# Seven products for both projections of the last two token tiles of a bilinear FFN

## The chip, the cores and the metric

One core of a Trainium2 chip runs the whole program. The metric is the device time of one execution in microseconds. Of the kernel before there are three timed runs: 325.77, 326.64 and 326.76 us, median 326.64. One further execution was taken by the profiler.

The core has a matrix engine (TensorE, PE in the profile), a vector engine (VectorE, DVE), a scalar engine (ScalarE, ACT), a general engine (GpSimd, POOL) and a queue engine (SyncE, SP) that issues transfers. Matmuls write to PSUM, eight banks of 128 partitions by 2 KB. VectorE and ScalarE read PSUM; in this kernel GpSimd works on SBUF only.

## The reference

Two stages, of which only the second is touched. The first is attention over 8 batches, 8 heads, 576 positions and head size 64, with a local mask for four heads and a strided mask for the other four. Its output, as a matrix x of 4608 tokens by 512, goes through a bilinear feed-forward layer:

```
a = x @ w_a          # 4608 x 512 times 512 x 1536
b = x @ w_b          # the same shape
out = (a * b) @ w_out   # 4608 x 1536 times 1536 x 512, float32
```

## The kernel before, in words

**Tiles and slots.** The tokens are cut into nine tiles of 512 (t = 0 to 8). A tile has sixteen slots: twelve for the blocks f = 0 to 11 of 128 features (`ffn_ab`), in which a and b of a block are made and multiplied into `pf[:, f]`, and four for the output product with w_out (`ffn_y` in tiles 0 and 1, `ffn_ys` in tiles 2 to 8). The attention of batch b + 1 is woven into the slots of the feed-forward tiles, and ends in the output slots of tile 6. Tiles 7 and 8 are feed-forward alone.

**Order.** The order of the work on each engine is the order in which the program is written out; nothing reorders it. A loop over the slots calls the slot's function, then what is due at that slot: entries put down with `do(slot, function, ...)`. Where a slot has such entries, a one-element copy on GpSimd (`pace`, line 1054) reads the slot's result, which holds GpSimd's queue back to about that slot.

**A plain block.** `ab_mm` (line 623) makes a and b in two PSUM banks by 4 matmuls of 512 columns each; ScalarE copies a to SBUF (line 644), and VectorE multiplies the copy with b out of PSUM into `pf` (line 647). The banks come from `mm_bank`: three banks with the tag mm and one with the tag tp, every fourth request going to tp. A bank of a tag is handed on in the order in which the banks of that tag came free. Four further banks serve the attention (`o` and `st`, two banks each).

**Seven products in place of eight.** The output product has been made this way since earlier versions: a 2 x 2 block matrix product with seven block products and some sums of blocks (Winograd's form of Strassen's scheme). `fast_w` makes the sums of w_out, `fast_s` (line 755) the sums of `pf` in `ps`, and `y_plan` (line 809) or, in the last tile, `y_tail` (line 838) makes the products 1 to 7 in three PSUM places X, Y, Z: 1, 6, 5 and 3 add up in X, 7 and 4 in Z, 2 stands in Y. ScalarE copies what stands there after 1, 7, 6, 5 and 3, VectorE adds after 4 and 2.

**The first projection in seven products.** Tiles 7 and 8 use the scheme for a alone as well, in four pairs of blocks each (`FAST_A`, `a_pair`, lines 700 to 735): a pair of blocks (2 x 128 features) by two halves of the tile (2 x 256 tokens) by two halves of the contraction. A product is then two matmuls of 256 columns (line 700). The b of the pair is made plainly (line 707), and VectorE multiplies both blocks at the end of the pair (line 712). The sums of w_a come from `wsum_make` (line 664; eight VectorE instructions of 768 elements, in tile 6's slots 2, 4, 6 and 8), the sums of x from `xsum_make` (line 674; one ahead of tile 7, three in its first slot, four in its output slots for tile 8). They stand in buffers that the attention has finished with. X of a pair is in the `st` or `o` banks.

**Columns of pf.** In tiles 2 to 8 the product is written into `pf` with its columns permuted, so that the two halves of the output scheme are blocks of sixteen tokens; the store puts the rows back in place.

Of the kernel before, what the change touches and what calls it, by code (L numbers as in the profile page):

```python
# [16 lines left out]
RS = 8  # L17
# [10 lines left out]
FAST_A = {7: (1, 2, 3, 4), 8: (0, 1, 2, 3)}  # L28
# [3 lines left out]
def kernel(  # L32
# [29 lines left out]
    pst = ctx.enter_context(tc.tile_pool(name="pst", bufs=1, space=bass.MemoryType.PSUM))  # L62
# [23 lines left out]
    vs_buf = [const.tile([NP, HL, RS, VW], BF16, name=f"vs{i}") for i in range(2)]  # L86
# [291 lines left out]
    def S_p(b, u):  # L378
# [3 lines left out]
        st = pst.tile([128, 2, 512], F32, tag="st", name="st")  # L382
# [243 lines left out]
    def ffn_ab(t, f, mid, ab=None):  # L626
        if f == 0:
            pfs[t] = fsb.tile([128, FD, TTOK], BF16, tag="pf", name="pf", bufs=1)
        pf = pfs[t]
        if f // 2 in FAST_A.get(t, ()):  # L630
            if f % 2 == 0:
                pairs[t, f // 2] = a_pair(t, f // 2)
            return next(pairs[t, f // 2])
        if ab is None:
            ab = [mm_bank([128, TTOK]) for _ in range(2)]
            if f == 0:

                late = 1 if t == 1 else 3
                ab_mm(t, f, ab, [kk for kk in range(KD) if kk != late], last=-1)
                ab_mm(t, f, ab, [late], first=-1, last=late)  # L640
            else:
                ab_mm(t, f, ab, range(KD), mid)
        a_sb = fsb.tile([128, TTOK], F32, tag="a_sb", name="a_sb")
        nc.scalar.copy(a_sb, ab[0])  # L644
        if t in FAST_Y:
            halves = lambda x: x.rearrange("p (a i s) -> p a i s", i=2, s=16)
            nc.vector.tensor_mul(pf[:, f, :].rearrange("p (i a s) -> p a i s", i=2, s=16), halves(a_sb), halves(ab[1]))  # L647
        else:
            nc.vector.tensor_mul(pf[:, f, :], a_sb, ab[1])  # L649
        return pf[:1, f, :1]  # L650

    wav = wa_sb.rearrange("p (j c) (g e m) -> p j c g e m", c=2, e=2, m=128)
    wsum_a = [flat.rearrange("p (c g m) -> p c g m", c=2, g=FG)
              for flat in [vl_buf[0].rearrange("p a b -> p (a b)")[:, 12 * 128 * z:12 * 128 * (z + 1)] for z in range(2)]
              + [t.rearrange("p a b c -> p (a b c)")[:, :12 * 128] for t in qz_pair[0]]]
    xsum = {t: qz_pair[1][t - 7].rearrange("p a b c -> p (a b c)")[:, :8 * HT].rearrange("p (n c m) -> p n c m", n=4, c=2)
            for t in FAST_A}

    def wsum_make(n):
        w, s_ = (lambda e, j: wav[:, j, :, :, e]), wsum_a  # L660
        a, b, op = ((w(1, 0), w(1, 1), ALU.add), (s_[0], w(0, 0), ALU.subtract), (w(0, 0), w(1, 0), ALU.subtract),
                    (w(0, 1), s_[1], ALU.subtract))[n]
        for c in range(2):
            nc.vector.tensor_tensor(s_[n][:, c], a[:, c], b[:, c], op=op)
# [11 lines left out]
    pairs = {}  # L676

    def a_pair(t, g):

        pf = pfs[t]  # L680
        pool, nm = ((pst, "st"), (psum4["o"], "o"))[g % 2]
        X = pool.tile([128, 2, 512], F32, tag=nm, name="ax")[:, 0, :HT]
        a = ([fsb.tile([128, TTOK], F32, tag="a_sb", name="a_sb") for _ in range(2)] if g % 2 == 0 else
             [t.rearrange("p h n -> p (h n)")[:, :2 * TTOK].bitcast(F32) for t in kT_buf[0]])
        got = {k: psum4[nm].tile([128, TTOK], F32, tag=nm, name="mm")
               for k, nm in zip((1, "Z", "Y", 0), (("mm", "mm", "tp", "mm"), ("tp", "mm", "mm", "mm"))[g % 2])}
        Z, Y = got["Z"][:, :HT], got["Y"][:, :HT]
        p7 = fsb.tile([128, HT], F32, tag="p7", name="p7")
        quarter = lambda e, k: a[e][:, HT * k:HT * (k + 1)]
        w = lambda e, j: (lambda c: wav[:, j, c, g, e])  # L690
        ws = lambda n: (lambda c: wsum_a[n][:, c, g])
        x = lambda j, k: (lambda c: x_part(t, j, k)[:, c])
        xs = lambda n: (lambda c: xsum[t][:, n, c])
        plan = {"1": (X, w(0, 0), x(0, 0)), "2": (Y, w(0, 1), x(1, 0)), "3": (X, ws(3), x(1, 1)), "4": (Z, w(1, 1), xs(3)),
                "5": (X, ws(0), xs(0)), "6": (X, ws(1), xs(1)), "7": (Z, ws(2), xs(2))}

        def P(k):
            bank, lhs, rhs = plan[k]
            for c in range(2):
                nc.tensor.matmul(bank, lhsT=lhs(c), rhs=rhs(c), start=k in "172" and c == 0, stop=c == 1, skip_group_check=True)  # L700

        x0 = TTOK * t % (XR * S)

        def b_mm(e, kks):
            f = 2 * g + e
            for kk in kks:
                nc.tensor.matmul(got[e], lhsT=wb_sb[:, kk, 128 * f:128 * (f + 1)], rhs=xT[:, kk, x0:x0 + TTOK],  # L707
                                 start=kk == 0, stop=kk == KD - 1)

        def mult(e):  # L710
            halves = lambda v_: v_.rearrange("p (a i s) -> p a i s", i=2, s=16)
            nc.vector.tensor_mul(pf[:, 2 * g + e, :].rearrange("p (i a s) -> p a i s", i=2, s=16),
                                 halves(a[e]), halves(got[e]))

        P("1")
        nc.scalar.copy(quarter(0, 0), X)
        b_mm(1, (0, 1, 2))
        P("6")
        nc.scalar.copy(quarter(1, 0), X)
        b_mm(1, (3,))  # L720
        P("7")
        nc.scalar.copy(p7, Z)
        P("2")
        nc.vector.tensor_tensor(quarter(0, 0), Y, quarter(0, 0), op=ALU.add)
        yield None
        P("5")
        nc.scalar.copy(quarter(1, 1), X)
        nc.gpsimd.tensor_tensor(quarter(1, 1), quarter(1, 1), p7, op=ALU.add)
        if (t, g - 1) in later:
            later.pop((t, g - 1))()  # L730
        b_mm(0, (0, 1))
        P("4")
        nc.vector.tensor_tensor(quarter(1, 0), Z, quarter(1, 0), op=ALU.add)
        P("3")
        nc.scalar.copy(quarter(0, 1), X)
        b_mm(0, (2, 3))
        mult(1)
        mult(0)
        yield pf[:1, 2 * g + 1, :1]

    later = {}
# [3 lines left out]
    def fast_s(t, n, gs):  # L745
# [6 lines left out]
        if (t, n) == (NT - 1, 2) and {gs.start, gs.start + 1} <= set(FAST_A[t]):  # L752
            later[t, gs.start] = lambda: nc.gpsimd.tensor_tensor(s[:, n], a, b, op=op)
            return
# [18 lines left out]
    def y_store(eng, t, y, i, q, n=slice(0, d_model)):  # L773
        rows = out[TTOK * t:TTOK * (t + 1), n].rearrange("(a i s q) c -> a s i q c", i=2, s=8, q=2)
        eng.dma_start(out=rows[:, :, i, q], in_=y[i][:, q, n])
# [18 lines left out]
    Y_ORDER = [(x[0], int(x[1])) for x in "10 11 70 71 60 61 40 41 50 51 20 21 30 31".split()]  # L794
    TAIL_ORDER = [(x[0], int(x[1])) for x in "10 70 60 11 40 50 71 30 61 20 51 41 31 21".split()]

    def y_plan(t):

        plan, y = products(t), y_bufs()
        bank = {x: mm_bank([128, 2, HN]) for x in "ZXY"}  # L800

        def store_half(i):
            rows = out[TTOK * t:TTOK * (t + 1)].rearrange("(a i s q) c -> a s i (q c)", i=2, s=8, q=2)
            nc.sync.dma_start(out=rows[:, :, i], in_=y[i].rearrange("p q c -> p (q c)"))

        for n, (k, q) in enumerate(Y_ORDER):
# [14 lines left out]
    def y_tail(t):  # L821

        plan, y = products(t), y_bufs()
        banks = [{x: mm_bank([128, HN]) for x in "ZXY"},
                 {"X": psum4["o"].tile([128, 2, 512], F32, tag="o", name="end")[:, 0, :HN],
                  "Z": pst.tile([128, 2, 512], F32, tag="st", name="end")[:, 0, :HN]}]
        for k, q in TAIL_ORDER:
# [4 lines left out]
            for n in cuts:  # L832
                if (q, k) == (1, "2"):
                    bank = mm_bank([128, 128])
# [10 lines left out]
                if k == "54"[q]:  # L845
                    y_store(nc.sync, t, y, 1, q)
                elif (q, k) == (0, "2"):
# [7 lines left out]
    def ffn_ys(t, j, mid):  # L855
# [9 lines left out]
        return (y[0][:1, 0, :1], None, y[1][:1, 0, HN:HN + 1], y[1][:1, 0, :1])[j]  # L865
# [36 lines left out]
    with tc.manual_schedule(engines={ENG.PE, ENG.SP, ENG.Pool, ENG.DVE, ENG.Activation}):  # L902
        early = ExitStack()
        open_psum(early, tp=2, sum=1, misc=1, o=2)
# [28 lines left out]
        for nm in ORDER:  # L933
# [26 lines left out]
            elif nm[0] == "F":  # L960
                f = int(nm[1])
                if nm[2] == "A":
                    if f == 1:
                        ab = pst.tile([128, 2, 512], F32, tag="st", name="ab")
# [10 lines left out]
        open_psum(ctx, mm=3, tp=1, o=1)  # L975
# [17 lines left out]
        for t in FAST_Y[:-1]:  # L993
# [7 lines left out]
        for b in range(FIRST_D, B):  # L1001
# [15 lines left out]
            for (z, nm, part), g in zip(((0, "k", 0), (0, "k", 1), (0, "q", 0), (0, "q", 1), (1, "k", 0), (1, "k", 1),  # L1017
                                         (1, "k", 2), (1, "q", 0), (1, "q", 1), (1, "q", 2)), gs):
                if (b, z, nm, part) != (FIRST_D, 0, "k", 1):
                    do(g0 + g, step_D, b, z, nm, part)  # L1020
        for n in range(4):
            do(16 * (NT - 3) + 2 * n + 2, wsum_make, n)
        do(16 * (NT - 2) - 1, xsum_make, NT - 2, 0)
        for n in (2, 1, 3):
            do(16 * (NT - 2), xsum_make, NT - 2, n)
        for n in range(4):
            do(16 * (NT - 2) + 12 + n, xsum_make, NT - 1, n)
# [10 lines left out]
        for g in range(FG):  # L1038
            for n in (2, 0, 1, 3):
                do(16 * (NT - 1) + 2 * g + 1, fast_s, NT - 1, n, slice(g, g + 1))  # L1040
        for t in FAST_Y[:-1]:
# [46 lines left out]
```

## Time and profile before

| what | us |
|---|---|
| timed runs | 325.77, 326.64, 326.76 (median 326.64) |
| the profiled execution, first to last instruction | 325.7 |
| tile 7: projections, then output product | 19.93 and 9.16 |
| tile 8: projections, then output product | 20.22 and 9.37 |
| from TensorE's end to the last instruction | 4.5 |

The page gives the profiled execution's span; it lies 0.9 us under the median of the timed runs, which also hold what lies around the span. In the profile's rows a start is given in microseconds from the span's start, then the duration, the engine, the line of the kernel and the tiles written and read. Matmuls overlap, so the time of one is read from the starts of many in a row. Instructions of VectorE and ScalarE overlap slightly as well: the next may start before the last has been written.

### The profile page before, as it was taken

The numbers are of one execution on the slowest core, as the hardware profiler recorded it, in microseconds if no ns is written. First come the engines' busy times: TensorE is split into PE (matmuls) and PEld (weight loads), VectorE is DVE, ScalarE is ACT, GpSimd is POOL, SyncE is SP. The second block draws the span as 40 slices with busy tenths as digits, with TensorE's granted clock in tenths as the row PEclk, the third lists the DMA queues.
The fourth block names the chain that finished last, engine by engine and source line by source line (L and its number), as shares of the span: only waits on it lengthen the run. The fifth ranks groups of instructions, "written<-read, shape, count | busy, mean of one in ns | idle before, by whom it ended". The sixth has DMA issues, their size and how long they took to land.

```text
span 325.7 us, 7440 instructions
## 1 busy us (share of the span) xinstructions
PE 319.1 (98%) x2672; PEld 209.0 (64%) x2672; DVE 258.2 (79%) x559; ACT 188.2 (58%) x328; POOL 160.6 (49%) x289
## 2 busy tenths in 40 slices
PE   8999999999999999999999999999999999999994
PEld 7754555445545577557999895559555966686573
DVE  6766786888878988898889888988999768837852
ACT  6763775468774476447654765467546655335441
POOL 8945936989848534762576338634113013103300
PEclk9999999999999999999999999999999999999998
DMA  9999999899999798999998999899245040004004
GB/s 159 141 203 202 202 187 172 190 170 146 123 218 139 134 99 96 108 202 149 107 112 170 196 102 100 163 187 118 46 99 147 20 129 1 2 0 131 0 3 129
DMA packets 111920, 40.73 MB, mean 125 GB/s; under 512 B 89868, under 2 KB 108940, under 8 KB 111884
## 3 DMA queue, kind: packets, MB, share of 16 engines
q0 software_dynamic: 85968, 19.48, 65.3%
q1 hardware_dynamic: 25772, 20.71, 27.4%
q8 instruction: 21, 0.34, 0.4%
q14 instruction: 15, 0.12, 0.1%
q10 hardware_dynamic: 144, 0.07, 0.1%
HBM read 39.51 MB, written 11.06 MB: 155 GB/s over the span
## 4 chain that ended last, share of the span: by engine, by line
PE 80%; DMA 8%; POOL 7%; DVE 1%; issue 1%; ACT 1%; POOLq 0%
PE mm L623 41%; PE mm L809 17%; PE mm L873 5%; DMA shared<-in_q_dram 4%; DMA vl<-in_v_dram 4%; PE mm L707 4%; PE st L388 4%; PE o L526 2%; PE ax L700 2%; POOL shared L197 2%; PE mm L838 2%; PE mm L700 2%; PE o L466 1%; PE end L838 1%; POOL wo_sb L255 1%
## 5 line engine op out<-in xcount | busy, mean ns | idle before, releaser
L623 PE MATMUL mm<-xT,wb_sb 128*128 128x512 bf16 (+1 forms) x408 | 93.7, 354 | 0.2 <-DMA wb_sb<-in_moe_w_b_dram 0.2
L623 PE MATMUL mm<-xT,wa_sb 128*128 128x512 bf16 (+1 forms) x408 | 93.7, 354 | 0.0
L644 ACT COPY a_sb<-mm 128x512 f32<-128x512 f32 x90 | 52.6, 585 | 53.9 <-PE mm L623 51.8
L623 PEld LDWEIGHTS <-wb_sb 128*128 128x128 bf16 x416 | 40.1, 98 | 37.1 <-DMA wb_sb<-in_moe_w_b_dram 0.9
L1054 POOL CAST pace<-pf 1x1 f32<-1x1 bf16 x83 | 25.3, 305 | 69.8 <-DVE pf L647 51.2
L647 DVE TENSOR_TENSOR pf<-a_sb,mm 128x512 bf16<-128x512 f32 x68 | 46.2, 680 | 9.2 <-PE mm L623 8.1
L623 PEld LDWEIGHTS <-wa_sb 128*128 128x128 bf16 x416 | 37.4, 98 | 24.0
L409 ACT ACTIVATE p<-st 72x576 bf16<-72x576 f32 (+1 forms) x56 | 36.4, 650 | 15.3 <-PE st L388 15.1
L542 DVE TENSOR_TENSOR xT<-o,xr 64x288 bf16<-64x288 f32 x48 | 21.4, 446 | 14.7 <-ACT xr L536 14.4
L809 PEld LDWEIGHTS <-ps 128*128 128x128 bf16 x288 | 28.0, 98 | 3.1
L786 ACT COPY y_sb<-mm 128x512 f32<-128x512 f32 (+1 forms) x28 | 15.5, 555 | 17.9 <-PE mm L809 15.3
L809 PE MATMUL mm<-wf,ps 128*128 128x256 bf16 x216 | 25.5, 273 | 0.0
L535 ACT ACTIVATE xr<-o 64x576 f32<-64x576 f32 x28 | 18.1, 647 | 12.3 <-PE o L526 12.0
L873 PE MATMUL mm<-wo_sb,pf 128*128 128x512 bf16 x96 | 23.4, 379 | 0.1
L243 POOL DMA_DIRECT2D vs<-in_v_dram x24 | 19.6, 818 | 5.1 <-PE mm L809 2.4
L809 PEld LDWEIGHTS <-pf 128*128 128x128 bf16 x216 | 20.3, 98 | 2.5 <-issue 0.2
L1054 POOL COPY pace<-y_sb 1x1 f32<-1x1 f32 x23 | 5.4, 233 | 33.2 <-DVE y_sb L784 19.8
L536 ACT ACTIVATE xr<-xr 64x576 f32<-64x576 f32 x28 | 19.1, 683 | 0.9
L212 POOL DMA_DIRECT2D ql<-in_q_dram x24 | 15.9, 664 | 6.3 <-DMA wo_sb<-in_moe_w_out_dram 4.6
L707 PE MATMUL mm<-xT,wb_sb 128*128 128x512 bf16 x64 | 19.0, 379 | 0.0
L809 PE MATMUL mm<-wo_sb,pf 128*128 128x256 bf16 x144 | 18.5, 273 | 0.1
L649 DVE TENSOR_TENSOR pf<-a_sb,mm 128x512 bf16<-128x512 f32 x22 | 14.9, 676 | 4.7 <-ACT a_sb L644 2.7
(189 smaller groups left out, 566.4 us busy)
## 6 DMA issues: line engine op xcount, KB each, us to landing
out_dram<-y_sb SPq DMA_DIRECT2D x12, 512.0 KB, 5.8
out_dram<-y_sb SPq DMA_DIRECT2D x11, 256.0 KB, 4.1
vl<-in_v_dram POOLq DMA_DIRECT2D x6, 384.0 KB, 8.2
kl<-in_k_dram POOLq DMA_DIRECT2D x24, 72.0 KB, 3.3
ql<-in_q_dram POOLq DMA_DIRECT2D x24, 72.0 KB, 3.2
vs<-in_v_dram POOLq DMA_DIRECT2D x24, 72.0 KB, 4.4
wo_sb<-in_moe_w_out_dram POOLq DMA_DIRECT2D x4, 384.0 KB, 9.3
natk<-in_k_dram POOLq DMA_DIRECT2D x20, 72.0 KB, 3.4
```

The source lines that it names most:

```text
L243: nc.gpsimd.dma_start(out=vs_buf[b % 2][:, h, :, 0:D], in_=v[b, HL + h].rearrange("(p r) d -> p r d", r=RS))
L409: nc.scalar.activation(p_flat(p)[:M, :2 * W].rearrange("p (i n) -> p i n", n=2 * n), st[:M].rearrange("p a (i n) -> p (a i) n", n=256)[:, ...
L535: nc.scalar.activation(r, sums, ACT.Ln)
L536: nc.scalar.activation(r, r, ACT.Exp, scale=-1.0)
L542: nc.vector.tensor_mul(dst.rearrange("d (p r) -> d p r", r=RS)[:, :, G * half:G * (half + 1)], o[:64, j, :W].rearrange("d (g p) -> d p g", ...
L623: nc.tensor.matmul(ps_[:, c0:c0 + n], lhsT=w[:, kk, 128 * f:128 * (f + 1)], rhs=xT[:, kk, x0:x0 + n], start=(kk == first and c0 == 0), sto ...
L644: nc.scalar.copy(a_sb, ab[0])
L647: nc.vector.tensor_mul(pf[:, f, :].rearrange("p (i a s) -> p a i s", i=2, s=16), halves(a_sb), halves(ab[1]))
L707: nc.tensor.matmul(got[e], lhsT=wb_sb[:, kk, 128 * f:128 * (f + 1)], rhs=xT[:, kk, x0:x0 + TTOK], start=kk == 0, stop=kk == KD - 1)
L809: nc.tensor.matmul(bank[b][:, q], lhsT=lhs(g, q), rhs=rhs(g), start=k in "172" and q == 0 and g == 0, stop=g == FG - 1, skip_group_check=True)
L873: nc.tensor.matmul(ybank[j], lhsT=pf[:, f, 128 * j:128 * (j + 1)], rhs=wo_sb[:, f], start=(f == 0), stop=(f == FD - 1))
L1054: nc.gpsimd.tensor_copy(pace, done)
```

## The change

Tiles 7 and 8 are made in halves of six blocks. In a half with the scheme, one pair of blocks is plain and the other two have **both** a and b by seven products. `JOINT` says which: tile 7's first half is all plain, its second has the plain pair 5 and the joint pairs 3 and 4; tile 8 has the plain pair 0 with the joint pairs 1 and 2, then 5 with 3 and 4. So a product is four matmuls of 256 columns, two for a and two for b side by side in one PSUM bank. After products 1, 7 and 6 ScalarE copies both at once (512 elements); after 2, 5 and 4 VectorE adds the bank to the copy (512 elements) and GpSimd multiplies a's half with b's half (256 elements) into `pf`; after 3 ScalarE copies a's half and VectorE multiplies it with b's out of PSUM (256). The two joint pairs (a and b in the order's names) and the plain pair (A0, B0, A1, B1) are woven in a written order.

With it come:

- `wsum_make` also makes the sums of w_b: eight more VectorE instructions, two each in tile 7's slots 0 to 3. The x sums of tile 7 move to its slots 2 and 3.
- The sums of `pf` (`fast_s`) are put down anew: in tile 7 in slots 3, 4, 7 and 8 and, for blocks 6 to 11, four 768-wide sums at the end of the second half; in tile 8 four of 256 and four of 512 elements over the first eight steps of the second half, and four of 768 at its end.
- The banks of `o` and `st` are given up at tile 7's second half and serve as Za, B, Zb and A; Ya, Yb and Xb are the mm banks, Xa is the tp bank.
- The output products of both tiles use those banks, in another order, and `pf` and the stores of both tiles are no longer permuted.
- `pace` does not act in the joint halves nor in the two tiles' output slots.

```diff
-FAST_A = {7: (1, 2, 3, 4), 8: (0, 1, 2, 3)}
+JOINT = {7: (None, (5, 3, 4)), 8: ((0, 1, 2), (5, 3, 4))}
...
+    def eight(nm, shape=(128, 2, HT)):
+        if not ends:
+            psums.close()
+            ends["pool"] = ctx.enter_context(tc.tile_pool(name="pend", bufs=1, space=bass.MemoryType.PSUM))
+            for x in ("Za", "B", "Zb", "A"):
+                eight(x)
+        pool, tag = {"Ya": (psum4["mm"], "mm"), "Yb": (psum4["mm"], "mm"), "Xb": (psum4["mm"], "mm"),
+                     "Xa": (psum4["tp"], "tp")}.get(nm, (ends["pool"], f"e{nm}"))
+        return pool.tile(list(shape), F32, tag=tag, name=f"e{nm}")
...
+    JOINT_ORDER = ("1a A0 B0 2a 1b 7a 6a 2b 7b 6b A1 5a 5b B1 4a 3a 4b 3b",
+                   "A0 1a 1b B0 7a 6a 7b 6b A1 2a 5a 2b 5b B1 4a 3a 4b 3b")
+
+    def joint(t):
...
+        for half, gs in enumerate(JOINT[t]):
+            if gs is None:
+                continue
+            plain, *gs = gs
+            banks = {x: eight(x) for x in "Ya Yb Xb Zb Xa Za".split()}
+            order = JOINT_ORDER[half].split()
+            for at_, (k, m) in enumerate(order):
+                if k in "AB":
+                    f = 2 * plain + int(m)
+                    if k == "A":
+                        ab = [eight("A", [128, TTOK]), eight("B", [128, TTOK])]
+                    ab_mm(t, f, ab, range(KD), ws=("AB".index(k),))
+                    if k == "A":
+                        a_sb = fsb.tile([128, TTOK], F32, tag="a_sb", name="a_sb")
+                        nc.scalar.copy(a_sb, ab[0])
+                    else:
+                        nc.vector.tensor_mul(pf[:, f, :], a_sb, ab[1])
+                else:
...
+                    for s in range(2):
+                        for c in range(2):
+                            w = wsum[s][lhs][:, c, g] if isinstance(lhs, int) else wviews[s][:, lhs[1], c, g, lhs[0]]
+                            x = xsum[t][:, rhs, c] if isinstance(rhs, int) else x_part(t, *rhs)[:, c]
+                            nc.tensor.matmul(bank[:, s], lhsT=w, rhs=x, start=k in "172" and s == 0 and c == 0, stop=c == 1,
+                                             skip_group_check=True)
...
+                    if k in "176":
+                        nc.scalar.copy({"1": s1, "7": s3, "6": s2}[k], bank)
+                    elif k == "3":
+                        nc.scalar.copy(c12, bank[:, 0])
+                        mult(nc.vector, 0, 1, c12, bank[:, 1])
+                    else:
+                        c, e, kk = {"2": (s1, 0, 0), "5": (s3, 1, 1), "4": (s2, 1, 0)}[k]
+                        nc.vector.tensor_tensor(c, bank, c, op=ALU.add)
+                        mult(nc.gpsimd, e, kk, c[:, 0], c[:, 1])
+                if half and JOINT[t][0] and at_ < 8:
+                    fast_s(t, at_ % 4, slice(0, 1) if at_ < 4 else slice(1, 3))
+                if (half, at_) == (1, len(order) - 1):
+                    for n in range(4):
+                        fast_s(t, n, slice(3, 6))
+                if at_ % 3 == 2:
+                    yield None
...
-    TAIL_ORDER = [(x[0], int(x[1])) for x in "10 70 60 11 40 50 71 30 61 20 51 41 31 21".split()]
+    Y_ORDERS = [[(x[0], int(x[1])) for x in o.split()] for o in
+                ("10 11 70 71 60 61 40 41 50 51 20 21 30 31", "10 11 20 21 60 61 70 71 50 51 40 41 30 31")]
+    TAIL_ORDER = [(x[0], int(x[1])) for x in "10 11 20 60 70 61 50 71 40 51 30 41 31 21".split()]
...
-                if k == "54"[q]:
+                if k == "4":
                     y_store(nc.sync, t, y, 1, q)
-                elif (q, k) == (0, "2"):
+                elif (q, k) == (0, "3"):
                     y_store(nc.sync, t, y, 0, q)
...
+        t7 = 16 * (NT - 2)
         for n in range(4):
-            do(16 * (NT - 3) + 2 * n + 2, wsum_make, n)
-        do(16 * (NT - 2) - 1, xsum_make, NT - 2, 0)
-        for n in (2, 1, 3):
-            do(16 * (NT - 2), xsum_make, NT - 2, n)
+            do(t7 - 16 + 2 * n + 2, wsum_make, 0, n, nc.vector)
+            do(t7 + n, wsum_make, 1, n, nc.vector)
+            do(t7 + (n + 4) // 2, xsum_make, NT - 2, n)
+            do(t7 + 3 + n // 2, fast_s, NT - 2, n, slice(0, 2))
+            do(t7 + 7 + n // 2, fast_s, NT - 2, n, slice(2, 3))
         for n in range(4):
-            do(16 * (NT - 2) + 12 + n, xsum_make, NT - 1, n)
+            do(t7 + 12 + n, xsum_make, NT - 1, n)
```

## The prediction

> **What bounds the kernel now.** I read the page's shares first, then the busy time by stage, the chain that ended last, and VectorE's timeline through the eighth and ninth tiles (t = 7 and 8). The page:
>
> ```profile
> span 325.7 us, 7440 instructions
> PE 319.1 (98%) x2672; PEld 209.0 (64%) x2672; DVE 258.2 (79%) x559; ACT 188.2 (58%) x328; POOL 160.6 (49%) x289
> ```
>
> TensorE (PE) is busy 98% of the span, so a change is worth what it takes off TensorE's stream, less the waits that it puts in. The busy time of four stretches (tile 7's projections, its output products, tile 8's projections, its output products); columns PE, weight loads, VectorE (DVE), ScalarE (ACT), GpSimd (POOL), clock, DMA:
>
> ```profile
> 262.49:282.42 19.93, 19.93 (x123) 11.74 (x121) 15.90 (x34) 10.37 (x25) 4.24 (x10) 1.00 0.18 54
> 282.42:291.58 9.16, 9.16 (x85) 8.21 (x84) 5.32 (x12) 2.35 (x4) 1.04 (x3) 1.00 0.00 0
> 291.58:311.80 20.22, 20.14 (x123) 11.66 (x121) 15.08 (x37) 10.27 (x25) 5.78 (x12) 1.00 0.17 53
> 311.80:321.17 9.37, 9.37 (x91) 8.20 (x89) 4.00 (x11) 3.72 (x10) 0.31 (x1) 1.00 0.21 52
> ```
>
> TensorE fills them at full clock, and VectorE is second with 15.90 of 19.93 us: there is little room on it. The chain prices the matmuls and shows tile 8's one real wait:
>
> ```profile
> 279.12 3.45 PE mm L623 x16
> 282.58 9.18 PE mm L809 x84
> 291.79 0.58 ACT y_sb L792
> 292.37 0.28 ACT a_sb L716
> 292.70 0.38 PE ax L700 x2
> ```
>
> A 512-column matmul costs 3.45/16 = 0.2156 us, a 256-column one 9.18/84 = 0.1093. Product 6 of tile 8's first pair waited for a ScalarE copy that stood behind the last output copy: the stage lasts 20.22 where its matmuls need 19.92 (below), so 0.30 us is waiting. VectorE's timeline:
>
> ```profile
> 240.06 1.02 DVE L664 TENSOR_TENSOR vl<-vl,wa_sb 128x768 bf16<-128x768 bf16 x2
> 241.00 0.42 DVE L755 TENSOR_TENSOR ps<-pf 128x512 bf16<-128x512 bf16 x1
> 264.82 0.69 DVE L647 TENSOR_TENSOR pf<-a_sb,mm 128x512 bf16<-128x512 f32 x1 [0.73 <-ACT a_sb L644]
> 265.42 0.42 DVE L674 TENSOR_TENSOR qz1l<-xT 128x512 bf16<-128x512 bf16 x1
> 265.76 0.88 DVE L674 TENSOR_TENSOR qz1l<-xT,qz1l 128x512 bf16<-128x512 bf16 x2
> 266.55 0.68 DVE L647 TENSOR_TENSOR pf<-a_sb,mm 128x512 bf16<-128x512 f32 x1
> ```
>
> Starts give what an instruction holds VectorE for: a weight sum 0.47 (two from 240.06 to 241.00), a 512-wide product 0.60 (264.82 to 265.42, written 0.69 after its start), a 512-wide bf16 sum 0.34 (265.42 to 265.76), or 0.46 if it needs the one before it.
>
> **The change part by part.**
>
> *Matmuls.* A plain pair of blocks is 16 x 0.2156 = 3.45 us, a pair with a alone by seven products 14 x 0.1093 + 8 x 0.2156 = 3.26, one with both by seven products 28 x 0.1093 = 3.06. Tile 7 goes from 2 plain + 4 a-alone (19.92) to 4 plain + 2 joint (19.92): nothing. Tile 8 goes from 19.92 to 2 plain + 4 joint = 19.14: **-0.78**. The 0.30 of waiting goes as well, since product 1 is now followed by 1.72 us of plain matmuls before a bank or a copy is needed again: **-0.30**. Output products: the same matmuls in another order.
>
> *VectorE in tile 7's first half.* New there: 8 weight sums, 4 of the x sums a little later than now, 4 sums of pf; the six products stay. The queue is in program order. From 264.82 (first product, unchanged): product 0 to 265.42, two weight sums to 266.36, product 1 to 266.96, weight sums to 267.90, product 2 (its matmuls end 267.66, start 0.27 later, as elsewhere) 267.93 to 268.53, x sums 0 and 1 to 269.33, weight sums to 270.27, product 3 to 270.87, pf sums 0 and 1 (the first waits for product 3's write, the second for the first) to 271.80, x sum 2 to 272.14, weight sums to 273.08, x sum 3 to 273.42, product 4 to 274.02, pf sums 2 and 3 to 274.70, product 5 from 274.70, written 275.39. TensorE needs 12 x 0.862 for the half: it is done about 272.83. VectorE is then 2.6 us behind.
>
> *Where that bites.* The joint half opens with A0 and 1a (0.86 + 0.44, to 274.13), both in banks that are free. 1b takes the third of the three mm banks, handed on in the order in which they came free: block 4's b, block 5's a, block 5's b. So 1b waits for product 5: 275.39 + 0.05 (a matmul that waits for VectorE starts that much after its end, as at 305.74) = 275.44. **+1.31**. Behind it in TensorE's queue is all else; ScalarE and GpSimd wait with it, and nothing later takes the time back, as TensorE has no gap. The sums of the row prices leave 0.1 either way.
>
> *The ends of the second halves.* The last products come each 0.44 us, VectorE's adds take 0.60: after B1 it does 4a, 3a, 4b, 3b late, then four 768-wide sums of pf (0.47 each, 0.55 to the write, by the weight sums' row). 3b's product is written 1.32 us after its matmuls end. Output product 2 writes that bank 1.31 after them: +0.06 with the latency. Its weights for block pair 4 come from GpSimd's multiplication of 4b, 0.72 long by the f32 addition of the same size (L728: 0.72 to 0.74; L753: 0.67): ready 1.8 after, +0.13. Both in each tile, +0.38; and in tile 8, whose sixth product comes sooner, 0.06 for the second sum: **+0.44**. GpSimd multiplying has no row: each 0.1 more than 0.72 costs 0.1 per tile. Below nothing can't be, as nothing starts sooner.
>
> *Middle of tile 8.* 1b of the second half needs 3b's bank of the first: written 303.74 in this run-down, wanted 303.93. Free, by 0.19 us. Nine ScalarE copies of about 0.5 us in a half of 9.6, and six GpSimd multiplications of 0.72, lie beside the matmuls; a joint bank is wanted again at the soonest 1.7 us after its last matmul, when its copy or add has long been made.
>
> *Queues.* SP's stores of tile 7 come after two and three slots of tile 8 as before and nothing waits for them. GpSimd's pace copies in tile 7's first half now stand ahead of no DMA. In the last tile the store of the first half's even rows moves from 2.6 us ahead of the last matmuls to 2.0, so 256 KB come closer to the last 512 KB. From the windows of the end (231 GB/s in the best of 318 to 320, 288 at 322 to 323) 256 KB take about 1 us, so between 0 and 0.35 us; I take **+0.10**, nearer to nothing, because the engines move at 0.67 to 0.91 there. No gain: the last three stores keep their order.
>
> *Sum:* -0.78 - 0.30 + 1.31 + 0.44 + 0.10 = **+0.77**. The profiled execution's span is 325.7; its sum would be 326.5. The median of the runs shown is 326.64, 0.9 above the span, and the difference is carried over: **327.4**. What this kernel's measurement can tell is about 0.3%, 0.98 us: forecast no change that can be told, on the slow side.
>
> **The rivals.**
>
> *The wait at 1b is not there* (VectorE catches up, or another bank falls to 1b). For it: if the weight sums cost half, 1.9 us less, the queue is done in time. Against it: each of the pairs of weight sums from 240 us on holds VectorE for 0.93 to 0.94. Without it: +0.77 - 1.31 = -0.54, 326.1.
>
> *GpSimd and VectorE get in each other's way (slower).* At the end of a second half the first 768-wide sum, with two inputs in SBUF, starts while GpSimd multiplies 4b, also out of SBUF. Now they overlap only with VectorE first:
>
> ```profile
> 268.55 0.72 POOL L728 TENSOR_TENSOR kT0s<-kT0s,p 128x256 f32<-128x256 f32 x1 [2.67 <-ACT kT0s L727]
> 271.55 0.41 DVE L755 TENSOR_TENSOR ps<-pf 128x512 bf16<-128x512 bf16 x1
> 271.80 0.74 POOL L728 TENSOR_TENSOR a_sb<-a_sb,p 128x256 f32<-128x256 f32 x1 [1.52 <-ACT a_sb L727]
> ```
>
> The second to come lost 0.02 us for 0.16 of overlap, against it. For it: the order GpSimd first has no row. If the sum had to wait, it would start 0.46 later; tile 7 hides that behind 21, tile 8 does not: +0.77 + 0.46 = +1.23, 327.9, and slower by the bound from 0.21 of those 0.46 on. The Trainium skill, "SBUF — State Buffer", section "Who interferes with whom", says that the one that issues second is blocked until the first ends. By that rule the time would be 327.9, by the row 327.4; the trace does not agree with it, since GpSimd would have lost 0.16 us at 271.80 and lost 0.02.
>
> *The last stores queue up.* The upper end of their bound, +0.35 for 0.10: +1.02, 327.7. For it: DMA is at 0.91 in the last full microsecond. Against it: 0.67 and 0.74 in the two before.
>
> **How the numbers follow.** Forecast 0.47, of which 0.38 inside the bound and 0.09 above it (GpSimd's multiplication, the thin 0.19 us). No wait at 1b 0.20: its middle is 0.44 short of the bound, and if the ends of the halves cost nothing either it is at the bound, so 0.10 faster and 0.10 the same. GpSimd against VectorE 0.20, slower. The stores 0.13, half and half: 0.06 the same, 0.07 slower. Together faster 0.10, same 0.54, slower 0.36. The range goes from no wait (326.1) less 0.2 for smaller ends, 325.9, to both of the slow rivals together (+0.77 + 0.46 + 0.25 = +1.48), 328.1.
>
> **What would show it.** In the profile after: tile 8's projections last 19.1 to 19.2 us, tile 7's 21.2; one gap of 1.2 to 1.4 us on TensorE 1.3 us into tile 7's second half, ended by VectorE's product of block 5; the weight sums and that product back to back; two gaps under 0.2 at the first output product 2 of each tile; GpSimd's multiplications near 0.72. Wrong if the gap at 1b is missing or over 1.5, if the 256-column matmuls run slower than 0.109 in the joint pairs, if GpSimd's multiplications take 1 us or more, or if a sum of pf stands waiting beside one of them.

## The result and the profile after

The changed kernel takes 324.95 us, median of 6 runs (324.64 to 325.64), beside 326.7 us for the kernel before on the same chip (6 runs, 325.77 to 326.95): 0.995 of it, with a 95% interval of 0.9934 to 0.9966. Three later series of runs, each beside the kernel before, gave 0.9964 [0.9950, 0.9978], 0.9963 [0.9950, 0.9975] and 0.9952 [0.9934, 0.9971]. So it is 1.2 to 1.8 us faster, where 327.4 us and no change were forecast.

The page's shares after:

```profile
span 323.9 us, 7434 instructions
PE 316.5 (98%) x2668; PEld 211.2 (65%) x2696; DVE 261.4 (81%) x555; ACT 187.2 (58%) x316; POOL 162.5 (50%) x285
```

The busy time by stage (the four stretches of the prediction, with the columns it names):

```profile
262.19:282.12 19.93, 19.82 (x121) 11.76 (x121) 16.90 (x37) 8.67 (x16) 4.39 (x9) 1.00 0.18 54
282.12:291.36 9.24, 9.24 (x87) 8.13 (x84) 6.62 (x15) 2.71 (x5) 1.46 (x2) 1.00 0.00 0
291.36:310.49 19.13, 18.97 (x143) 14.09 (x144) 13.08 (x27) 10.21 (x20) 7.13 (x10) 1.00 0.14 56
310.49:320.22 9.73, 9.44 (x92) 8.13 (x89) 5.73 (x14) 4.09 (x11) 1.46 (x2) 1.00 0.14 51
```

The last stretch ends here by the matmuls' spacing. With the last matmul's modelled end, as in the table of before, it is 310.49 to 320.39, and 3.51 us are left to the last instruction. Stage by stage:

| stage | before | after | forecast | measured |
|---|---|---|---|---|
| start of tile 7 | 262.49 | 262.19 | 0 | -0.30 |
| tile 7, projections | 19.93 | 19.93 | +1.31 | 0.00 |
| tile 7, output product | 9.16 | 9.24 | +0.19 | +0.08 |
| tile 8, projections | 20.22 | 19.13 | -1.08 | -1.09 |
| tile 8, output product | 9.37 | 9.90 | +0.25 | +0.53 |
| TensorE's end to the last instruction | 4.53 | 3.51 | +0.10 | -1.02 |
| sum | 325.7 | 323.9 | +0.77 | -1.80 |

The first row can't be put down to the change. In four profiled executions of the changed kernel the last tile's output product begins at 310.49, 309.81, 310.16 and 310.29, while it is 48.30 us from the start of tile 7 to there in all four; and the kernel before, with nothing but the rows of its last stores changed (an experiment below), began tile 7 at 261.54, where the profile of the kernel before has 262.49. Without that row the change is worth -1.50; the medians of the four series say -1.2 to -1.8. Two rows hold the surprise: the wait in tile 7 that isn't there, and the end.

### The profile page after: what moved, and what is told of

Its sections match the earlier page's. It is cut to its first block, busy times and chain, and to the rows that moved or that the text cites. A ratio compares the mean times of both kernels' runs of the same rounds, so it can differ in the third digit from the quotient of the medians.

```text
span 323.9 us, 7434 instructions
## 1 busy us (share of the span) xinstructions
PE 316.5 (98%) x2668; PEld 211.2 (65%) x2696; DVE 261.4 (81%) x555; ACT 187.2 (58%) x316; POOL 162.5 (50%) x285
## 4 chain that ended last, share of the span: by engine, by line
PE 79%; DMA 10%; POOL 5%; DVE 3%; issue 1%; ACT 0%; POOLq 0%; DVEq 0%
PE mm L624 40%; PE mm L821 14%; PE mm L883 5%; DMA vl<-in_v_dram 4%; DMA wb_sb<-in_moe_w_b_dram 4%; PE st L389 4%; PE o L527 2%; DMA shared<-in_q_dram 2%; PE eYa L821 2%; PE eA L624 2%; POOL shared L198 2%; PE o L467 1%; PE eXb L731 1%; PE eXa L731 1%; PE eB L624 1%
## 5 line engine op out<-in xcount | busy, mean ns | idle before, releaser
L624 PE MATMUL mm<-xT,wb_sb 128*128 128x512 bf16 (+1 forms) x397 | 91.3, 353 | 0.4
L624 PE MATMUL mm<-xT,wa_sb 128*128 128x512 bf16 (+1 forms) x383 | 89.9, 352 | 0.7
L624 PEld LDWEIGHTS <-wb_sb 128*128 128x128 bf16 x432 | 41.8, 98 | 37.3 <-issue 0.2
L624 PEld LDWEIGHTS <-wa_sb 128*128 128x128 bf16 x432 | 39.0, 98 | 24.8
L648 DVE TENSOR_TENSOR pf<-a_sb,mm 128x512 bf16<-128x512 f32 x60 | 40.7, 679 | 6.4 <-PE mm L624 6.1
L650 DVE TENSOR_TENSOR pf<-a_sb,mm 128x512 bf16<-128x512 f32 x28 | 19.0, 677 | 5.2 <-ACT a_sb L645 3.7
L821 PE MATMUL mm<-wf,ps 128*128 128x256 bf16 x180 | 21.3, 273 | 0.0
L763 DVE TENSOR_TENSOR ps<-pf 128x512 bf16<-128x512 bf16 (+2 forms) x42 | 18.2, 434 | 0.6
L735 POOL TENSOR_TENSOR pf<-vl 128x256 bf16<-128x256 f32 x9 | 6.5, 730 | 23.9 <-DVE vl L744 23.9
L213 POOL DMA_DIRECT2D kl<-in_k_dram x24 | 16.0, 666 | 4.8 <-issue 4.0
L794 ACT COPY y_sb<-mm 128x512 f32<-128x512 f32 x20 | 11.7, 585 | 10.3 <-PE mm L821 10.2
```

The source lines that it names most:

```text
L213: nc.gpsimd.dma_start(out=t[32 * h:32 * h + 32], in_=src[b, h].rearrange("(i y) d -> y i d", y=32))
L624: nc.tensor.matmul(ps_[:, c0:c0 + n], lhsT=w[:, kk, 128 * f:128 * (f + 1)], rhs=xT[:, kk, x0:x0 + n], start=(kk == first and c0 == 0), sto ...
L821: nc.tensor.matmul(bank[b][:, q], lhsT=lhs(g, q), rhs=rhs(g), start=k in "172" and q == 0 and g == 0, stop=g == FG - 1, skip_group_check=True)
```

## The experiments

### Which bank the first products of tile 7 got

VectorE is as late in the changed kernel as the prediction had it. Its timeline at the end of tile 7's first half, after ScalarE's copy of block 5's a:

```profile
271.89 0.59 ACT L645 COPY a_sb<-mm 128x512 f32<-128x512 f32 x1 [1.14 <-PE mm L624]
...
271.83 1.02 DVE L666 TENSOR_TENSOR natk<-wb_sb,vs 128x768 bf16<-128x768 bf16 x2
272.77 0.42 DVE L676 TENSOR_TENSOR qz1l<-xT,qz1l 128x512 bf16<-128x512 bf16 x1
273.10 0.68 DVE L650 TENSOR_TENSOR pf<-a_sb,mm 128x512 bf16<-128x512 f32 x1
273.70 0.42 DVE L763 TENSOR_TENSOR ps<-pf 128x512 bf16<-128x512 bf16 x1
274.04 0.42 DVE L763 TENSOR_TENSOR ps<-pf,ps 128x512 bf16<-128x512 bf16 x1
274.37 0.68 DVE L650 TENSOR_TENSOR pf<-a_sb,mm 128x512 bf16<-128x512 f32 x1
```

Block 5's product starts at 274.37; 274.70 was forecast, and the whole tile lies 0.30 sooner. TensorE's timeline at the same place:

```profile
272.55 1.03 PE L624 MATMUL eA<-xT,wa_sb 128*128 128x512 bf16 x4
273.41 0.38 PE L731 MATMUL eXa<-xT,wa_sb 128*128 128x256 bf16 x2
273.63 0.38 PE L731 MATMUL eXa<-xT,wb_sb 128*128 128x256 bf16 x2
273.85 0.38 PE L731 MATMUL eXb<-xT,wa_sb 128*128 128x256 bf16 x2
```

Product 1b (eXb) follows 1a without a gap and runs before VectorE has even begun to read block 5's b. So its bank was not block 5's b. In the program as built Xb stands where block 5's **a** was, Ya where block 4's b was and Yb where block 5's b was. The three are requested at once, in the order Ya, Yb, Xb, but that is not the order in which they got their banks. The banks come free in the order block 5's a (ScalarE's copy, done at 272.48), block 4's b (VectorE's product, 273.78), block 5's b (275.05), and they went to the names in the order in which these are first written: Xb in 1b, Ya in 2a, Yb in 2b. So the rule that a bank is handed on in the order of coming free holds here; what takes its turn is the first write, not the request. The next kernel's program fits as well: there the three banks were block 3's b, block 5's a and block 4's b, and they went to Xb, Ya and Yb. Block 5's b goes to 2b, nine steps after 1b in the written order.

To see whether the price of the wait was right, it was brought about. One skipped turn in the counter that gives every fourth request to the tp bank puts block 5's b into the bank that 1a takes:

```diff
@ ffn_ab
+            if (t, f) == (NT - 2, FD // 2 - 1):
+                used[0] += 1
```

> The changed kernel, but block 5 of tile 7 takes its two banks one request later, so that its b stands in the tp bank and product 1a of the first joint pair has to wait for VectorE's product of block 5. Theory (VectorE's queue is as late as was worked out, and only the bank kept it off TensorE): that product is written near 275.1 in the changed kernel's time, 1a would start at 273.4, so a gap of 1.6 to 1.7 us on TensorE ahead of 1a, ended by VectorE, and the time is 324.95 + 1.65 = 326.6. Rival (VectorE's lateness there costs TensorE nothing whichever bank it reads): no gap, 324.9 to 325.0.

Measured: 326.6 us (10 runs), 1.0004 [0.9993, 1.0015] of the kernel before (326.4 beside it). TensorE's timeline of this kernel:

```profile
272.13 1.03 PE L624 MATMUL eA<-xT,wa_sb 128*128 128x512 bf16 x4
274.69 0.38 PE L733 MATMUL eXa<-xT,wa_sb 128*128 128x256 bf16 x2 [1.53 <-DVE pf L652]
```

The late product is a wait of 1.69 us here (from 273.00, where A0's matmuls end by their spacing, to 274.69), and by the ratios the kernel loses 1.3 to 1.8 us, all that the change had gained. The wait was priced rightly, and put at a bank that didn't have it.

The second kernel keeps that bank and makes the sums of w_b in tile 6, where those of w_a are made:

```diff
-            do(t7 + n, wsum_make, 1, n, nc.vector)
+            do(t7 - 16 + 2 * n + 3, wsum_make, 1, n, nc.vector)
```

> The same as the run with block 5's b in the tp bank, but b's weight sums are made in tile 6 (slots 3, 5, 7 and 9) and not in tile 7's first half. Theory (the eight weight sums are what makes VectorE late): 3.8 us leave its queue, block 5's product is written 0.9 us after its matmuls end, and the gap ahead of 1a is 0.1 to 0.3 us; time 324.9 to 325.3. Rival (the shifted banks cost the time by themselves, or VectorE is late for other reasons): the gap stays above 1 us, 326 or more.

Measured: 326.93 us (10 runs), 1.0018 [1.0007, 1.0030]. In tile 7 it does what was expected: A0 starts at 273.66, 1a at 274.69, a gap of 0.17. The time is not what was expected, 324.9 to 325.3. Tile 7 starts at 263.30, 1.5 us later than in the kernel beside it (261.77), and from 250 to 260 us TensorE waits for VectorE ahead of tile 6's output product, while in the kernel without the early sums no wait of TensorE in that window names VectorE:

```profile
PEld L823 <- DVE pf L650: 1.3, 1, 1.3
PE mm L823 <- DVE pf L650: 1.0, 1, 1.0
```

VectorE has no idle time from 236 to 257 us there, with eight more instructions of 0.47 us each. The output product of tile 6 now waits for one of VectorE's last products of tile 6, where 1a had waited for block 5's: the wait moved, it didn't go.

### Where the end got shorter

The store queue over the last 14 us, first before:

```profile
q1 hardware_dynamic: 720, 0.98, 26.3%
...
out_dram<-y_sb SPq DMA_DIRECT2D x3, 256.0 KB, 2.8
...
out_dram<-y_sb SPq DMA_DIRECT2D x1, 64.0 KB, 2.5
```

and after:

```profile
q1 hardware_dynamic: 720, 0.98, 19.8%
...
out_dram<-y_sb SPq DMA_DIRECT2D x3, 256.0 KB, 2.0
...
out_dram<-y_sb SPq DMA_DIRECT2D x1, 64.0 KB, 1.9
```

The same 720 packets and 0.98 MB took 0.263 x 14 x 16 / 720 = 0.082 us of an engine each before, and 0.062 after; each store lands 0.6 to 0.9 us sooner. These are means. In the traces' packet records the median packet of 2 KB takes much the same, 0.084 and 0.086 us; but of the 384 such packets 168 took over 0.12 us before, 0.178 on average, and none did after. One thing that differs is where the rows go. A store writes 128 rows, every second one. Before they lie in sixteens (eight rows written, then a gap of sixteen, over the whole tile); after they lie in one run of 256 rows. Two kernels undo and do this part alone: the changed kernel with the old rows, and the kernel before with the new ones. In both the last tile's rows end up in the wrong places of the output, since the columns of `pf` stay as they were; what is stored, and in which order, stays too.

```diff
@ last_rows_old, against the changed kernel (before_rows_new is the reverse, against the kernel before)
-        rows = out[TTOK * t:TTOK * (t + 1), n].rearrange("(i p q) c -> p i q c", i=2, q=2)
-        eng.dma_start(out=rows[:, i, q], in_=y[i][:, q, n])
+        rows = out[TTOK * t:TTOK * (t + 1), n].rearrange("(a i s q) c -> a s i q c", i=2, s=8, q=2)
+        eng.dma_start(out=rows[:, :, i, q], in_=y[i][:, q, n])
```

> The changed kernel, but the last tile's stores go to the rows of the kernel before (blocks of sixteen rows for each half), so the last tile's rows land in other places. Theory A (the rows of the stores set how fast the last 0.8 MB drain): from the last matmul to the end of the span 4.7 us as before instead of 3.7, the last stores land after 2.5 to 2.9 us instead of 1.9 to 2.0, time 324.95 + 0.8 to 1.0 = 325.8 to 325.9. Theory B (the order and moment of the stores does): 3.7 us, 324.9 to 325.0. Theory C (it differs from run to run): neither, the spread stays.

> The kernel before, but the last tile's stores go to the rows of the changed kernel (a half of the tile is 256 rows in a run), so the last tile's rows land in other places. Theory A (rows): 0.8 to 1.0 us less than before, 325.7 to 325.9 where before has 326.7. Theory B (order and moment of the stores) and theory C (chance): as before, 326.5 to 326.9.

Measured, beside 326.4 us for the kernel before: the changed kernel with the old rows 326.0 us (9 runs), 0.9984 [0.9974, 0.9994]; the kernel before with the new rows 325.9 us (12 runs), 0.9984 [0.9970, 0.9998]. The stores of the changed kernel with old rows:

```profile
q1 hardware_dynamic: 720, 0.98, 24.7%
...
out_dram<-y_sb SPq DMA_DIRECT2D x3, 256.0 KB, 2.9
```

and of the kernel before with new ones:

```profile
q1 hardware_dynamic: 720, 0.98, 19.8%
...
out_dram<-y_sb SPq DMA_DIRECT2D x3, 256.0 KB, 2.0
```

In the packet records 139 of the 384 took over 0.12 us in the first, none in the second. From TensorE's end to the last instruction it is 4.26 us with the old rows and 3.51 with the new in the changed kernel (3.49 to 3.54 in its four profiles), 4.53 and 3.77 in the kernel before: 0.75 and 0.76 us for the rows, in both, as theory A has it. By the medians it is 0.7 to 1.1 in the one and 0.5 in the other. The other 0.27 of the 1.02 came with the rest of the change; the new order of the products and their stores is the likely cause, and was not tried apart. Why some packets take twice as long with the rows in sixteens is open too.

### The wait ahead of product 6 in the last tile

The changed kernel was run once more beside the next two, on the same chip. The letters of the theories below are those of the expectations.

> The changed kernel once more, unedited, so that the two runs beside it have it on the same chip. Both theories: 1.4 to 1.8 us under the kernel before of this call; in the last tile a wait of about 0.4 us ahead of output product 6, and the first 768-wide sum of pf at about 0.79 us beside GpSimd's multiplication.

Measured: 325.09 us (8 runs; the kernel before 326.49). Its tail has the two waits of the first profile. TensorE, of the changed kernel's first profile:

```profile
311.80 0.91 PE L848 MATMUL eXb<-wo_sb,pf 128*128 128x256 bf16 x6
312.55 0.49 PE L848 MATMUL eYa<-wf,ps 128*128 128x256 bf16 x3
313.32 0.50 PE L848 MATMUL eYa<-wf,ps 128*128 128x256 bf16 x3 [0.29 <-DVE ps L763]
313.67 0.60 PE L848 MATMUL eYb<-wf,ps 128*128 128x256 bf16 x4
```

Six matmuls take 0.655. Product 2 (eXb) takes 0.75 and product 6 (the two lines of eYa) 1.12: 0.09 and 0.46 of waiting, the second for VectorE's sums. VectorE and then GpSimd at that place:

```profile
311.37 0.41 DVE L735 TENSOR_TENSOR pf<-p,eXb 128x256 bf16<-128x256 f32 x1
311.88 0.79 DVE L763 TENSOR_TENSOR ps<-pf 128x768 bf16<-128x768 bf16 x1
312.71 0.56 DVE L763 TENSOR_TENSOR ps<-ps,pf 128x768 bf16<-128x768 bf16 x1
```

```profile
311.53 0.73 POOL L735 TENSOR_TENSOR pf<-vs 128x256 bf16<-128x256 f32 x1 [0.20 <-DVE vs L744]
```

The first sum takes 0.79 us, its like 0.55, and it starts while GpSimd multiplies. To tell a mutual hindrance from a sum that is long of itself, GpSimd's multiplication was cut to 16 columns. The rest of its quarter of `pf` is set to zero when the half begins, so a part of a * b is left out for two blocks:

```diff
+            if (t, half) == (NT - 1, 1):
+                for g in gs:
+                    nc.gpsimd.memset(pf[:, 2 * g + 1, :HT], 0.0)
...
-                        mult(nc.gpsimd, e, kk, c[:, 0], c[:, 1])
+                        if (t, half, k) == (NT - 1, 1, "4"):
+                            at16 = slice(HT * kk, HT * kk + 16)
+                            nc.gpsimd.tensor_tensor(pf[:, 2 * g + e, at16], c[:, 0, :16], c[:, 1, :16], op=ALU.mult)
+                        else:
+                            mult(nc.gpsimd, e, kk, c[:, 0], c[:, 1])
```

> The changed kernel, but in the ninth tile's second half GpSimd's two multiplications of product 4 cover 16 of 256 columns (the rest of that quarter of pf is set to zero at the start of the half), so they are done before VectorE's first 768-wide sum. That leaves out part of a * b for two blocks. Theory L (GpSimd ahead of VectorE holds VectorE's two-input sum up): the first 768-wide sum of the last tile falls from 0.79 to about 0.55 us, the wait ahead of product 6 from 0.44 to about 0.20, and the 0.09 ahead of product 2 goes; the time is 0.2 to 0.35 us under the unedited changed kernel. Theory V (the sum is long of itself, for instance because it waits for the write of the product before it): the sum stays at 0.75 to 0.80, the wait ahead of product 6 at 0.4, and only the 0.09 goes; the time is within 0.1 us of the unedited one.

Measured: 324.88 us (6 runs), 0.21 under the changed kernel beside it, by medians whose intervals overlap; the profile is the surer witness. VectorE's first sums:

```profile
312.36 0.56 DVE L770 TENSOR_TENSOR ps<-pf 128x768 bf16<-128x768 bf16 x1
312.95 0.56 DVE L770 TENSOR_TENSOR ps<-ps,pf 128x768 bf16<-128x768 bf16 x1
```

The sum takes 0.56: for its length theory L holds and theory V falls. The 0.09 is gone, and product 6 waits 0.32 in place of 0.46, so 0.23 of 0.55 were GpSimd's. That is less than theory L expected, which left a wait of 0.20. The rest is in the same lines: the sums don't come 0.47 apart. The first starts 0.51 after 3b's product rather than 0.33 (311.85 to 312.36), as it reads what that writes (0.51 in the lines of the changed kernel too), and the second 0.59 after the first, whose result it reads.

Three versions tried to use this. The first takes both halves of product 2 ahead of product 6 and cuts product 3 in two at the end in place of product 2:

```diff
-    TAIL_ORDER = [(x[0], int(x[1])) for x in "10 11 20 60 70 61 50 71 40 51 30 41 31 21".split()]
+    TAIL_ORDER = [(x[0], int(x[1])) for x in "10 11 20 21 60 61 70 71 50 51 40 41 30 31".split()]
...
```

> A version meant to beat both. The changed kernel with the last tile's output products in the order of the tile before it (both halves of product 2 ahead of 6 and 7, so that TensorE has 0.66 us more work that needs no sum of pf), product 3 of the odd rows cut in two at the end instead of product 2, and the odd rows' left columns stored 2.6 us ahead of the end. Theory W (the wait ahead of product 6 is for the sums alone): that wait goes, TensorE ends 0.3 to 0.45 us sooner; with half as much data (128 KB in place of 256) in the last two stores the drain after the last matmul falls from 3.7 to 3.2 to 3.5; 324.1 to 324.6 us, 0.4 to 0.8 under the unedited changed kernel. Theory D (the drain is a fixed latency of the last store): the drain stays at 3.6 to 3.7, and the gain is the 0.3 to 0.45 of the wait. Theory M (the wait only moves to another product): nothing gained.

Measured: 325.4 us (11 runs), 0.9961 [0.9949, 0.9974]; no gain. The wait ahead of product 6 is gone, but TensorE's last two lines are

```profile
318.23 0.50 PE L845 MATMUL eXa<-wo_sb,ps 128*128 128x128 bf16 x6
319.08 0.49 PE L845 MATMUL eXa<-wo_sb,ps 128*128 128x128 bf16 x6 [0.35 <-ACT y_sb L800]
```

The second cut writes the bank out of which ScalarE copies the first (318.76, 0.27 long) and starts 0.52 after the first cut's matmuls end (318.56). The wait moved, as theory M has it, though to a copy and not to a sum. The next version leaves product 3 whole and lets ScalarE and VectorE copy half of it each:

> As the version before it, but product 3 of the odd rows is whole at the end, so that no matmul writes a bank that is being copied; after it ScalarE copies its left 128 columns and VectorE its right 128, and each half is stored (64 KB) from its own queue. Theory B (the 0.52 us ahead of the second cut was ScalarE's copy out of the same bank): no wait of TensorE in the last tile but the 0.09 at product 2, output products from first to last matmul 9.2 to 9.3 us in place of 9.73 to 9.79, the drain after the last matmul 3.6 to 3.8; 324.4 to 324.7 us, 0.4 to 0.6 under the unedited changed kernel. Theory D2 (the two copies or the two stores disturb each other): the drain is 4.1 or more and the gain is gone.

Measured: 325.38 us (5 runs), 0.9960 [0.9948, 0.9971], with the changed kernel beside it at 325.25. The output product is 9.25 us long as expected, but the time is not (324.4 to 324.7). VectorE's copy waits for ScalarE's (319.42 to 319.69) and starts at 319.72, and from the first output matmul (309.97) to the end (323.2) it is 13.23, against 13.39 to 13.44 in four executions of the changed kernel. The last version has VectorE copy it all, and the even rows' products ahead of the odd rows':

> As the version before it, with two edits: after the whole product 3 of the odd rows VectorE alone copies all 256 columns (0.42 us by a 256-wide sum, and no second copy behind ScalarE's out of the same bank), and the even rows' products come ahead of the odd rows' as in the changed kernel (6 7 of the even, 6 of the odd, and so on), so that the 256 KB stores of the even rows start one or two products sooner. Theory E (the end is the last copy plus a fixed 3.2 us, as in the runs so far: 320.39 to 323.6, 320.01 to 323.2): first output matmul to last instruction 9.25 + 0.04 + 0.42 + 3.2 = 12.9 us, against 13.4 in the unedited changed kernel and 13.23 in the version before it; 324.5 to 324.8 us. Theory Q (the engines that move the stores are the limit, since they are at 0.99 for the last 3 us): the end doesn't follow the copy, 13.2 or more, 324.9 to 325.2 us.

> The version before it unedited, to see whether its 324.77 us holds against the changed kernel, whose medians in four calls were 324.95 to 325.31 at 0.9950 to 0.9964 of the kernel before. By the spans (13.22 us from the first output matmul of the last tile to the end, against 13.4) it is worth 0.2 us: ratio to the kernel before 0.9945 to 0.9958. If the 0.9927 of the call before was right, 0.993 again.

Measured: 324.77 us (6 runs), 0.9927 [0.9903, 0.9950], then 324.99 us (7 runs), 0.9954 [0.9937, 0.9970]; the changed kernel beside the first of these 325.31. From the first output matmul to the end it is 13.22 (310.08 to 323.3) and 13.19, where theory E had 12.9. In the first the last copy ended at 319.95, 9.87 us after the first output matmul where theory E's sum has 9.71, and the end came 3.35 us later, not 3.2. So E falls, by 0.16 and 0.15; the second fits theory Q, but that the transfer engines set the end is not shown. By the spans it gains 0.2 us on the changed kernel, which the timed runs can't tell.

## Why the prediction was wrong

- *Matmuls and the wait in tile 8*, -0.78 - 0.30: right. 19.13 us measured, 19.14 worked out.
- *VectorE in tile 7's first half*: right, to 0.03 us at its sixth product.
- *Where that bites*, +1.31: wrong, and the main failure. The step put block 5's b under 1b by reading the requests as the order in which banks change hands. They change hands in the order of the first writes, so the bank that came free last went to the name written last, and the wait at 1b was 0.00 us. The rival "the wait at 1b is not there" named this very reason ("another bank falls to 1b"), but had only 0.20, because what was argued against it was VectorE's lateness, which says nothing of the bank. And that rival alone would have given 326.1, still above what was measured.
- *The ends of the second halves*, +0.44: measured +0.61, and put differently: 0.08 in tile 7 for 0.19, 0.53 in tile 8 for 0.25. The 0.06 for the bank was there in neither tile (product 2 starts without a gap, at 283.43 and 311.80), and in tile 8 the 0.13 for GpSimd's weights was 0.09. What was mis-sized in tile 8 is "0.06 for the second sum": 0.46 measured. About 0.14 of it is GpSimd in VectorE's way (0.46 less 0.32), and about 0.3 is that each sum waits for the write before it (0.18 and 0.12), where the working had counted 0.47 from start to start.
- *The rival of GpSimd and VectorE* holds as a mechanism, not as an outcome: VectorE lost 0.24 us in the last tile where 0.46 was priced.
- *Queues*, +0.10 with "No gain: the last three stores keep their order": wrong by 1.12. The step looked at when the stores start and how many bytes they move. That the rows were no longer permuted stood in the change, and was not asked for its price; 0.75 of it is shown by two runs to be the rows.

The two failed steps make -1.31 - 1.12 = -2.43 and the ends +0.17, which is the -2.27 between +0.77 and -1.50 to 0.01.

The weighing of the rule needs mending as well. The row it rested on was GpSimd's 0.74 for 0.72 at 0.16 us of overlap, read as "not blocked". With GpSimd first, VectorE's 768-wide sum of the last tile lost 0.24 of 0.38 us of overlap (311.88 to 312.26). The changed kernel has two more such pairs:

```profile
283.14 0.72 POOL L735 TENSOR_TENSOR pf<-vs 128x256 bf16<-128x256 f32 x1 [0.19 <-DVE vs L744]
301.76 0.73 POOL L735 TENSOR_TENSOR pf<-vs 128x256 bf16<-128x256 f32 x1 [0.21 <-DVE vs L744]
```

```profile
283.50 0.78 DVE L763 TENSOR_TENSOR ps<-pf 128x768 bf16<-128x768 bf16 x1
301.92 0.71 DVE L763 TENSOR_TENSOR ps<-pf 128x256 bf16<-128x256 bf16 x1
```

The same sum in tile 7 lost 0.23 of 0.36, and a 256-wide one at 301.92 lasted 0.71 for 0.29 and lost 0.42 of 0.57. The loss is the overlap less about 0.14 each time, and 0.02 of 0.16 fits the same line. A longer overlap with VectorE first had stood in the trace of before, GpSimd's one-element copy and VectorE beside it:

```profile
243.77 1.57 POOL L1054 CAST pace<-pf 1x1 f32<-1x1 bf16 x1 [1.45 <-DVE pf L647]
246.03 0.17 POOL L1054 CAST pace<-pf 1x1 f32<-1x1 bf16 x1 [0.69 <-DVE rc L474]
```

```profile
243.57 0.45 DVE L427 TENSOR_TENSOR p<-p,mask_s 72x576 int16<-72x576 int16 x1
243.95 1.02 DVE L664 TENSOR_TENSOR qz0l<-wa_sb 128x768 bf16<-128x768 bf16 x2
244.89 0.41 DVE L755 TENSOR_TENSOR ps<-ps,pf 128x512 bf16<-128x512 bf16 x1
245.22 0.68 DVE L647 TENSOR_TENSOR pf<-a_sb,mm 128x512 bf16<-128x512 f32 x1
```

A copy that takes 0.17 elsewhere lasts 1.57, to 245.34, as long as VectorE runs four instructions in a row with both inputs in SBUF, and ends as soon as one with an input in PSUM follows. In the kernel with the early sums of w_b three such copies last 1.55 beside the same kind of row (239.29, 244.09 and 248.89). That agrees with the rule of the Trainium skill, "SBUF — State Buffer", section "Who interferes with whom", that whichever of the two issues first keeps the other out entirely. The prediction's sentence that the trace does not agree with it was wrong; its row was too short an overlap to tell.

## What to carry to other kernels

Before a wait is priced at a buffer, find out which buffer the built program gives to which name; a lateness that is worked out to 0.03 us is worth nothing if it stands at another bank. A change in the layout of a transfer is a change in its price even where its bytes, packets and order stay: cost the stores after the last matmul by their landing time for each layout, as all of it is on the path. And to weigh a rule of contention against a trace, look for the longest overlap in it, not for the nearest kind of instruction.

## What the runs showed of the hardware

- Stores of 128 rows, every second one, took 0.077 to 0.082 us of an engine per packet and landed after 2.5 to 2.9 us with the rows in sixteens, and 0.062 us and 1.9 to 2.1 us with the rows in one run, at the same 720 packets and 0.98 MB. The median 2 KB packet was much the same (0.084 and 0.086 to 0.087 us); with the rows in sixteens 139 and 168 of 384 took over 0.12 us, with one run none.
- With both inputs in SBUF, four of VectorE's instructions in a row kept a copy of GpSimd's out for the whole row (0.17 became 1.57 us), and GpSimd's multiplication out of SBUF kept VectorE out too (0.55 became 0.79, 0.29 became 0.71); recorded durations overlapped by about 0.14 us without a loss.
